# Attention over a cache with a gated unit: the split of the query rounds around the gate, and how four rows of w_o are shared among the DMA engines

## The chip, the cores and the metric

The kernel runs on one core of a Trainium2 chip. The core has five engines, each with its own queue of instructions: TensorE (PE in the profile, with weight loads as PEld), VectorE (DVE), ScalarE (ACT), GpSimd (POOL) and SyncE (SP). They work side by side and wait for each other through semaphores. Loads from device memory are issued by SP and ScalarE and carried out by 16 DMA engines. [...]

The metric is the device time of one execution in microseconds (us). The kernel before took 687.47 us, the median of three runs (687.0 to 690.81).

## What is computed

One token x of 512 values is normalized; xn then goes two ways. One is attention for 32 heads of 128 values over a cache of 8192 positions, the other a small gated unit whose result scales the attention's:

```python
def _A_ref(x, k_cache, v_cache, wq, wo):
    q = (x @ wq).reshape(B, Sq, H, Dh).transpose(0, 2, 1, 3)
    scores = jnp.einsum("bhqd,bhkd->bhqk", q, k_cache) * (Dh ** -0.5)
    p = _softmax(scores, axis=-1)
    o = jnp.einsum("bhqk,bhkd->bhqd", p, v_cache)
    return o.transpose(0, 2, 1, 3).reshape(B, Sq, H * Dh) @ wo
...
    xn = _layernorm(x, axis=-1)
    s = _A_ref(xn, A_k_cache, A_v_cache, A_wq, A_wo)
    g = _silu(_B_ref(xn, B_w_gate, B_w_up, B_w_down))   # (sigmoid(xn Wg) * (xn Wu)) Wd
    return x + s * g
```

All values are float32. The cache of keys and that of values are 128 MiB each; w_q and w_o are 8 MiB each. Every byte is used once, so the kernel is a stream of some 294 MB with little arithmetic on it.

## The kernel before

**Slots.** Three large slots of on-chip memory, A, B and C, hold what is loaded, one after another. C has w_q first, then the values of each pair of heads, and w_o at the end. A has the gated unit's weights first, then the keys of the odd pairs. B has the keys of the even pairs, and at the end the values of the last pair. A load into a slot can be issued only when the slot's last reader is done. Every load of the large slots is issued by SP, in program order, and its DMA queue works them off in that order.

**The beginning.** SP issues w_q (line 148), w_gate, w_up, w_down and the keys of pair 0 in two halves (152 to 156). ScalarE issues x twice and the last 96 rows of w_down (`wr`, 174). VectorE normalizes x. TensorE then computes all queries in eight rounds of 512 columns (`queries`, line 234): a round is four products with w_q that add up in one PSUM bank, and ScalarE copies it to `q_all` with two copies, one for each half of the partitions (245). A round yields the queries of two pairs of heads. Four rounds (banks 0 to 3) come ahead of the gated unit, four (banks 4 to 7) behind it.

Between them lies the gate. VectorE sums the weighted rows of w_gate and of w_up (`weighted`, 221); TensorE turns each of the two sums from a row over the partitions into a column (258, into the banks `turned`), ScalarE applies the sigmoid (263), VectorE multiplies (`hid`, 266) and sums the weighted rows of w_down (269 to 272). TensorE waits for ScalarE's last copy of the first rounds (276), adds up over the partitions into `g_ps` (bank 3, line 279), and ScalarE applies the sigmoid to `g_row` (283). The silu's other factor, `g_ps` itself, is multiplied in later by VectorE (367), behind the first pair's scores.

Two loads hang on this. The keys of pair 1 go into slot A and wait for the gate's last matmul (`sp.wait_ge(s_pe.sem, n_gate)`, 359). The values of pair 0 go into slot C and wait for the last round of queries (`sp.wait_ge(s_q, nq)`, 369).

**The pairs.** For each of the 16 pairs of heads VectorE computes the scores in two halves (`scores`, 295: a product with the query in place, 307, and a sum, 309), TensorE and VectorE find the maximum, ScalarE the exponentials (`softmax`, 317), and TensorE multiplies them with the values (`pair`, 336; line 350) into bank `po`, bank 0. SP issues the next keys when the scores have read the slot, the next values when `po` is done. `busy` (332) issues matmuls whose result nobody reads, into the gate's bank.

**The end.** When the values of pair 14 are used, SP issues w_o into slot C, in five transfers of all 128 partitions, each with its own semaphore (382):

```python
WO = ((0, 16), (16, 24), (24, 29), (29, 31), (31, 32))
...
for (r0, r1), c in zip(WO, d_wo):
    c.by(sp.dma_start(wo_t[:, r0:r1, :], wo.rearrange("(p r) e -> p r e", r=RW)[:, r0:r1, :]), 16)
```

Partition p holds 32 rows of w_o, each 2 KB; "rows 0 to 16" are the first 16 of each partition. TensorE waits for each transfer in turn (410) and multiplies its rows with the normalized attention `o_all`: rows 0 to 24 into one bank (414), which ScalarE copies (423) and TensorE folds in (427), and rows 24 to 32 into another (418). VectorE multiplies by `g_row` (431) and adds x (433), and SP sends the result out (435).

Of the kernel before, what the change touches and what calls it, by code (L numbers as in the profile page):

```python
# [9 lines left out]
P = 128  # L10
# [15 lines left out]
def kernel(  # L26
# [12 lines left out]
    pe, dve, act, pool, sp = nc.tensor, nc.vector, nc.scalar, nc.gpsimd, nc.sync  # L39
    _, H, S, Dh = k_cache.shape  # L40
# [5 lines left out]
    KT = D // P  # L46
    NG = 4
    GP = P // NG
    GC = D // NG
    SCALE = float(Dh) ** -0.5  # L50
    FP = F // P
    FL = F - FP * P
    QT = 512
    RW = H * Dh // P
# [17 lines left out]
    q_all = put("q_all", NP * Dh).rearrange("p (n d) -> p n d", d=Dh)  # L72
# [5 lines left out]
    ones = put("ones", P)  # L78
    x_row = put("x_row", GC)
    g_row = put("g_row", GC)  # L80
# [20 lines left out]
    xnb = o1.rearrange("p (k m) -> p k m", m=P)  # L101
# [4 lines left out]
    wq_t = C.rearrange("p (k c) -> p k c", k=KT)  # L106
    wo_t = C.rearrange("p (r e) -> p r e", e=D)

    psum = nc.alloc_psum_tensor("psum", [P, 8 * QT], F32).ap()
    bank = [psum[:, i * QT:(i + 1) * QT] for i in range(8)]  # L110
    po, pt, pm, g_ps, acc, fold_ps, o_ps, oTl = bank


    sems = []
# [1 line left out]
    def semaphore(name):  # L116
        sems.append(nc.alloc_semaphore(name))
        return sems[-1]

    names = "x xr wg wu wd wr wq ka k0 k1 kb va vb".split()  # L120
    d = {n: Count(semaphore(f"d_{n}")) for n in names}
    WO = ((0, 16), (16, 24), (24, 29), (29, 31), (31, 32))
    d_wo = [Count(semaphore(f"d_wo{i}")) for i in range(len(WO))]
    d_v = semaphore("d_v")
    s_dve, s_act, s_pe, s_pool = (Count(semaphore(n)) for n in ("s_dve", "s_act", "s_pe", "s_pool"))
# [48 lines left out]
    d["wr"].by(act.dma_start(wd_rest[:FL, :], w_down[FP * P:, :]), 16)  # L174
    dve.memset(st[:, 6:7], EPS)
    dve.memset(rs2, 0.0)
    for b in (4, 5):
        dve.memset(bank[b][:, :FP + 1], 0.0)
    dve.wait_ge(s_pool.sem, 2)
    for g in range(NG):  # L180
# [47 lines left out]
    n_xnb = s_dve.by(dve.tensor_copy(xnb, xn.rearrange("p (k o) -> p k o", o=1).to_broadcast([P, KT, P])))  # L228


    nq = H // NG
    n_qc = []

    def queries(lo, hi):
        with nc.Fori(lo, hi, engines=[pe.engine]) as t:
            for k in range(KT):
                m = pe.matmul(psum[:, bass.ds(t * QT, QT)], xnb[:, k, :], wq_t[:, k, bass.ds(t * QT, QT)],  # L237
                              start=(k == 0), stop=(k == KT - 1))
            m.then_inc(s_q, 1)
        for t in range(lo, hi):  # L240
            act.wait_ge(s_q, t + 1)
            pairs = slice(t * NG // 2, (t + 1) * NG // 2)
            for a in range(2):
                r = slice(a * HALF, (a + 1) * HALF)
                c = act.copy(q_all[r, pairs, :], bank[t][r, :].rearrange("p (n a d) -> p n a d", a=2, d=Dh)[:, :, a, :])
            n_qc.append(s_act.by(c))

    pe.wait_ge(d["wq"].sem, 16)
    pe.wait_ge(s_dve.sem, n_xnb)
    queries(0, nq // 2)  # L250

    turned = [bank[nq // 2 + a][:, :FP + 1] for a in range(2)]
    for a, (name, t) in enumerate((("wg", wg_t), ("wu", wu_t))):
        dve.wait_ge(d[name].sem, 16)
        weighted(t[:, 0, :], lambda k: t[:, k, :], lambda k: xn[:, k:k + 1], KT)
# [1 line left out]
        for i in range(FP):  # L257
            m = pe.matmul(turned[a][:, i:i + 1], t[:, 0, i:FP * P:FP], ones[:, 0:1], start=True, stop=True)
        m = pe.matmul(turned[a][:FL, FP:FP + 1], t[:, 0, FP * P:F], ones[:, 0:1], start=True, stop=True)
        n = s_pe.by(m)  # L260
# [12 lines left out]
                                             op0=ALU.mult, op1=ALU.add))  # L273
    pool.wait_ge(s_dve.sem, n_wr)
    n_prz = s_pool.by(pool.memset(prz.rearrange("p j a -> p (j a)"), 0.0))
    pe.wait_ge(s_act.sem, n_qc[-1])
    pe.wait_ge(s_dve.sem, n_wr)
    for g in range(NG):
        m = pe.matmul(g_ps[g * GP:g * GP + 1, :GC], ones[:, 0:1], wd_t[:, 0, g * GC:(g + 1) * GC],
                      start=True, stop=True)  # L280
    n_gate = s_pe.by(m)
    act.wait_ge(s_pe.sem, n_gate)
    n_gs = s_act.by(act.activation(g_row, g_ps[:, :GC], AF.Sigmoid))
    act.wait_ge(s_pool.sem, n_prz)
    queries(nq // 2, nq)


    def load_k(n, parts=1):
# [6 lines left out]
    def scores(n):  # L295
        kt = k_slot(n).rearrange("p (j d) -> p j d", d=Dh)
        s = sc[n % 2]
        h = NB // 2
        q = q_all[:, n:n + 1, :].to_broadcast([P, h, Dh])
        first = {0: d["ka"], NP - 1: d["kb"]}.get(n)  # L300
        if first:
            dve.wait_ge(first.sem, 16)
        for i in range(2):
            if i == bool(first):
                dve.wait_ge(k_sem(n).sem, 16 * (n // 2 + 1))
            part = kt[:, i * h:(i + 1) * h, :]
            s_dve.by(dve.tensor_mul(part, part, q))  # L307
            self_wait()
            s_dve.by(dve.reduce_sum(s[:, i * h:(i + 1) * h], part, axis=AX.X))  # L309
        k_free[n] = s_dve.n  # L310
        self_wait()
        dve.reduce_max(mx[:, 0:1], s, axis=AX.X).then_inc(s_rm, 1)
        dve.wait_ge(s_pt, n + 1)
        dve.reduce_max(mx[:1, 2:4], pt[:1, :P].rearrange("p (a m) -> p a m", a=2), axis=AX.X).then_inc(s_am, 1)  # L314
# [16 lines left out]

    def busy(count):
        for _ in range(count):
            pe.matmul(g_ps, ones, q_all[:, :QT // Dh, :], start=True, stop=True)

    def pair(v, waits, keep=(0, 0)):
        busy(keep[0])
# [23 lines left out]
    for n in range(NP):  # L361
        if n % (NG // 2) == 0:
            dve.wait_ge(s_act.sem, n_qc[n // (NG // 2)])
        scores(n)
        if n == 0:
            dve.wait_ge(s_act.sem, n_gs)
            s_dve.by(dve.tensor_mul(g_row, g_row, g_ps[:, :GC]))
        softmax(n)
    sp.wait_ge(s_q, nq)
    for n in range(NP - 1):  # L370
# [7 lines left out]
    for name, c in (("va", slice(0, SLOT // 2)), ("vb", slice(SLOT // 2, SLOT))):  # L378
        d[name].by(sp.dma_start(B[:, c], rows_of(v_src, NP - 1)[:, c]), 16)
    sp.wait_ge(s_po, NP - 1)  # L380
    for (r0, r1), c in zip(WO, d_wo):
        c.by(sp.dma_start(wo_t[:, r0:r1, :], wo.rearrange("(p r) e -> p r e", r=RW)[:, r0:r1, :]), 16)  # L382

    pe.wait_ge(s_act.sem, n_qc[-1])
    with nc.Fori(0, NP - 1, engines=[pe.engine], head_slot={pe.engine: 0}):
# [13 lines left out]
    n = s_dve.by(dve.transpose(o_turn, o_norm))  # L399
    pe.wait_ge(s_dve.sem, n)  # L400
    n = s_pe.by(pe.matmul(o_ps[:, :RW], turn, o_turn, start=True, stop=True))
    busy(1)
    dve.wait_ge(s_pe.sem, n)
    n = s_dve.by(dve.tensor_copy(o_all, o_ps[:, :RW]))
# [2 lines left out]
    pe.wait_ge(s_dve.sem, n)  # L407
    FOLD = WO[1][1]
    for (r0, r1), c in zip(WO, d_wo):
        pe.wait_ge(c.sem, 16)  # L410
        for r in range(r0, r1):
            if r < FOLD:
                g = r % NG
                m = pe.matmul(fold_ps[g * GP:g * GP + 1, :], o_all[:, r:r + 1], wo_t[:, r, :],
                              start=(r < NG), stop=(r >= FOLD - NG))
            else:
                for g in range(NG):
                    m = pe.matmul(acc[g * GP:g * GP + 1, :GC], o_all[:, r:r + 1],  # L418
                                  wo_t[:, r, g * GC:(g + 1) * GC], start=(r == FOLD), stop=(r == RW - 1))
        if r1 == FOLD:  # L420
            n = s_pe.by(m)
            act.wait_ge(s_pe.sem, n)
            n_f = s_act.by(act.copy(o1, fold_ps))
        if r1 == WO[2][1]:
            pe.wait_ge(s_act.sem, n_f)
            for g in range(NG):
                pe.matmul(acc[g * GP:g * GP + 1, :GC], sel, o1[:, g * GC:(g + 1) * GC], start=False, stop=False)  # L427
    n = s_pe.by(m)
# [4 lines left out]
    n = s_dve.by(dve.tensor_add(res, res, x_row))  # L433
# [35 lines left out]
```

## Time and profile before

| | |
|---|---|
| median of three runs | 687.47 us (687.0 to 690.81) |
| the profiled execution | 687.28 us |
| its span, first to last instruction | 685.4 us |
| moved by the DMA engines | 293.74 MB, mean 429 GB/s |
| TensorE, VectorE, ScalarE busy | 36%, 86%, 6% of the span |
| mean granted TensorE clock | 0.659 of full speed |

The profile comes from one execution. A row of its timeline has the start and length of a group of instructions in us, the engine (a "q" behind it means the engine's queue, where loads are issued), the line of the program, the operation, what it writes and reads, how many there are, and in brackets how long the engine sat idle before it and what ended that. A row of a table by stretches of time has the stretch and its length, the busy time of each engine with the number of its instructions, the granted clock of TensorE, the mean busy share of the 16 DMA engines and the rate at which they moved data. A packet counts in the stretch in which it starts, so shares over short stretches swing around their mean. A row on DMA issues has the size and the time from issue to landing.

### The profile page before, as it was taken

The page shows a single profiled execution, that of the slowest core. Times are in us where ns is not written, and L with a number is a line of the kernel's source. Part 1 is how long each engine was busy: PE and PEld are TensorE (multiplying, and loading weights), DVE is VectorE, ACT ScalarE, POOL GpSimd, SP SyncE. Part 2 cuts the span into 40 slices and gives each one's busy share as a digit, 9 for nine tenths or more (in the row PEclk, how much of TensorE's full clock was granted, in tenths as well). Part 3 has the DMA queues.
Part 4 walks back from the last instruction along what each step waited for, and adds up shares of the span by engine and source line. Part 5 has one row for each costly group of instructions (what it writes and reads, how often), then busy time and mean ns, then how long its engine had stood idle before and what let it go on. Part 6 is the DMA issues. An engine that isn't in the chain of part 4 may idle for free. (4 is left out here: it accounts for less than half of the span.)

```text
span 685.4 us, 3572 instructions
## 1 busy us (share of the span) xinstructions
PE 245.0 (36%) x1502; PEld 92.5 (14%) x1502; DVE 588.5 (86%) x145; ACT 41.5 (6%) x135; POOL 1.7 (0%) x10
## 2 busy tenths in 40 slices
PE   1595315050412405050422406060422406050486
PEld 0272101010110101010110101010110101010132
DVE  2259999999999999898989899898989899899930
ACT  0010110000000000000010100000010100000010
POOL 0000000000000000000000000000000000000000
PEclk9976856575665657575565757565665756565699
DMA  8999999999999999999999999999999999999996
GB/s 370 419 439 429 437 451 440 432 432 432 433 428 432 428 428 444 444 436 436 432 436 428 432 428 428 436 448 440 428 440 432 432 428 432 428 423 449 425 433 292
DMA packets 6501, 293.74 MB, mean 429 GB/s; under 512 B 760, under 2 KB 768, under 8 KB 1120
## 3 DMA queue, kind: packets, MB, share of 16 engines
q1 hardware_dynamic: 6344, 293.48, 99.1%
q10 hardware_dynamic: 152, 0.20, 0.1%
q8 instruction: 3, 0.05, 0.0%
q14 instruction: 2, 0.02, 0.0%
HBM read 293.67 MB, written 0.00 MB: 428 GB/s over the span
## 5 line engine op out<-in xcount | busy, mean ns | idle before, releaser
L307 DVE TENSOR_TENSOR slot<-slot,q_all 128x8192 f32<-128x8192 f32 x32 | 277.8, 8682 | 21.6 <-DMA slot<-in_A_k_cache_dram 21.6
L309 DVE TENSOR_REDUCE sc<-slot 128x64 f32<-128x8192 f32 x32 | 278.0, 8686 | 1.1
L350 PE MATMUL psum<-slot,prz 128*8 128x512 f32 x1024 | 143.9, 725 | 241.6 <-PEq L134 241.6
L350 PEld LDWEIGHTS psum<-slot,prz 128*8 128x8 f32 x1024 | 29.9, 102 | 342.0 <-issue 341.4
L339 PE MATMUL psum<-ident,mx 128*1 128x128 f32 x32 | 9.2, 387 | 119.4 <-PEq L134 119.4
L237 PE MATMUL psum<-slot,o 128*128 x64 | 32.1, 666 | 9.8 <-DMA slot<-in_A_wq_dram 9.8
L327 ACT COPY o<-psum 128x512 f32<-128x512 f32 x16 | 9.4, 586 | 397.6 <-PE psum L350 397.6
L355 PE MATMUL psum<-pick,o 128*128 128x2 f32 x128 | 16.4, 250 | 12.8 <-PEq L134 12.8
L355 PEld LDWEIGHTS psum<-pick,o 128*128 128x128 f32 x128 | 15.5, 191 | 27.2 <-issue 27.2
L339 PEld LDWEIGHTS psum<-ident,mx 128*1 128x1 f32 x32 | 1.8, 80 | 121.8 <-issue 121.8
L237 PEld LDWEIGHTS psum<-slot,o 128*128 128x128 f32 x64 | 13.6, 217 | 27.1 <-issue 27.1
L344 PE MATMUL psum<-rs,ones 128*128 128x2 f32 x32 | 8.7, 342 | 22.3 <-PEq L134 22.3
L222 DVE TENSOR_SCALAR slot<-slot,xn 128x1376 f32<-128x1376 f32 x2 | 1.9, 936 | 15.5 <-DMA slot<-in_B_w_gate_dram 15.0
L314 DVE TENSOR_REDUCE mx<-psum 1x2 f32<-1x128 f32 x16 | 4.4, 278 | 12.1 <-PE psum L339 12.1
L323 ACT ACTIVATE prz<-sc,mx 64x128 f32<-64x128 f32 x32 | 13.0, 406 | 0.7
L431 DVE TENSOR_TENSOR sc<-g_row,psum 128x128 f32<-128x128 f32 x1 | 0.3, 290 | 13.1 <-PE psum L418 13.1
L319 ACT ACTIVATE mx<-psum 128x2 f32<-128x2 f32 x16 | 2.8, 173 | 143.2 <-PE psum L341 143.2
L341 PE MATMUL psum<-mx,ones 1*128 1x2 f32 x32 | 8.6, 336 | 7.4 <-PEq L134 7.4
L344 PEld LDWEIGHTS psum<-rs,ones 128*128 128x128 f32 x32 | 7.8, 305 | 23.9 <-issue 23.9
L225 DVE SCALAR_TENSOR_TENSOR slot<-slot,xn 128x1376 f32<-128x1376 f32 x6 | 9.9, 1652 | 0.2
L395 DVE RECIPROCAL heads<-heads 128x32 f32<-128x32 f32 x1 | 0.4, 355 | 11.1 <-ACT heads L329 11.1
L341 PEld LDWEIGHTS psum<-mx,ones 1*128 1x128 f32 x32 | 7.7, 297 | 14.7 <-issue 14.7
(67 smaller groups left out, 84.0 us busy)
## 6 DMA issues: line engine op xcount, KB each, us to landing
slot<-in_A_k_cache_dram SPq DMA_DIRECT2D x4, 4096.0 KB, 45.5
slot<-in_A_v_cache_dram SPq DMA_DIRECT2D x2, 4096.0 KB, 37.5
slot<-in_A_wo_dram SPq DMA_DIRECT2D x1, 4096.0 KB, 20.7
slot<-in_B_w_gate_dram SPq DMA_DIRECT2D x1, 2752.0 KB, 28.2
slot<-in_B_w_up_dram SPq DMA_DIRECT2D x1, 2752.0 KB, 34.3
slot<-in_B_w_down_dram SPq DMA_DIRECT2D x1, 2560.0 KB, 39.8
slot<-in_A_wo_dram SPq DMA_DIRECT2D x1, 2048.0 KB, 25.2
slot<-in_A_wo_dram SPq DMA_DIRECT2D x1, 1280.0 KB, 27.7
```

The source lines that it names most:

```text
L225: s_dve.by(dve.scalar_tensor_tensor(acc, t(k), col(k), acc, op0=ALU.mult, op1=ALU.add))
L237: m = pe.matmul(psum[:, bass.ds(t * QT, QT)], xnb[:, k, :], wq_t[:, k, bass.ds(t * QT, QT)], start=(k == 0), stop=(k == KT - 1))
L307: s_dve.by(dve.tensor_mul(part, part, q))
L309: s_dve.by(dve.reduce_sum(s[:, i * h:(i + 1) * h], part, axis=AX.X))
L314: dve.reduce_max(mx[:1, 2:4], pt[:1, :P].rearrange("p (a m) -> p a m", a=2), axis=AX.X).then_inc(s_am, 1)
L323: e = act.activation(prz[r, :, a], sc[n % 2][r, :], AF.Exp, bias=mx[r, 4 + a:5 + a], scale=SCALE, accum_out=rs2[r, a:a + 1])
L327: act.copy(o1, po).then_inc(s_o1, 1)
L339: pe.matmul(pt[:1, :P], mx[:, 0:1], ident, start=True, stop=True).then_inc(s_pt, 1)
L341: pe.matmul(pm[:, 0:2], ones[:1, :], mx[:1, 2:4], start=True, stop=True).then_inc(s_pm, 1)
L344: pe.matmul(oTl[:, 2:4], ones, rs2, start=True, stop=True)
L350: m = pe.matmul(po[g * GP:g * GP + 2 * ROWS, :], prz[:, j * ROWS:(j + 1) * ROWS, :], v[:, j * QT:(j + 1) * QT], start=(j < NG), stop=(j >= ...
L355: m = pe.matmul(oTl[:, 0:2], o1[:, b * Dh:(b + 1) * Dh], pick[:, 2 * b:2 * b + 2], start=(b == 0), stop=(b == ROWS - 1))
```

## The change

Two things are changed.

The queries: three rounds come ahead of the gate (banks 0 to 2), five behind it (banks 1 to 5, through the new argument `first`). The gate's sums go to bank 0, `po`, instead of bank 3, the columns of the two turned sums to banks 6 and 7 instead of 4 and 5, and the matmuls of `busy` to bank 3, now called `idle`. TensorE's wait for the last copy ahead of the gate is removed. The product of `g_row` and `g_ps` moves from behind the first pair's scores to the middle of them, ahead of their second half.

w_o: the first transfer has rows 0 to 12 of all 128 partitions instead of rows 0 to 16. Rows 12 to 16 follow in five more transfers: one of partitions 0 to 80, then four of twelve partitions each (80 to 92, 92 to 104, 104 to 116, 116 to 128). With five partitions per engine in the first and one in each of the others, that is nine partitions on each of twelve DMA engines, and five on each of the other four. All six count on the first transfer's semaphore, and TensorE waits for the sum.

```diff
-    po, pt, pm, g_ps, acc, fold_ps, o_ps, oTl = bank
+    po, pt, pm, idle, acc, fold_ps, o_ps, oTl = bank
+    g_ps = po
...
+    FEW = 4
     WO = ((0, 16), (16, 24), (24, 29), (29, 31), (31, 32))
...
-    for b in (4, 5):
+    for b in (6, 7):
         dve.memset(bank[b][:, :FP + 1], 0.0)
...
-    nq = H // NG
+    nq, n0 = H // NG, 3
...
-    def queries(lo, hi):
+    def queries(lo, hi, first):
         with nc.Fori(lo, hi, engines=[pe.engine]) as t:
             for k in range(KT):
-                m = pe.matmul(psum[:, bass.ds(t * QT, QT)], xnb[:, k, :], wq_t[:, k, bass.ds(t * QT, QT)],
-                              start=(k == 0), stop=(k == KT - 1))
+                m = pe.matmul(psum[:, bass.ds(t * QT - (lo - first) * QT, QT)], xnb[:, k, :],
+                              wq_t[:, k, bass.ds(t * QT, QT)], start=(k == 0), stop=(k == KT - 1))
...
-    queries(0, nq // 2)
-
-    turned = [bank[nq // 2 + a][:, :FP + 1] for a in range(2)]
+    queries(0, n0, 0)
+
+    turned = [bank[6 + a][:, :FP + 1] for a in range(2)]
...
-    pe.wait_ge(s_act.sem, n_qc[-1])
     pe.wait_ge(s_dve.sem, n_wr)
...
-    queries(nq // 2, nq)
+    queries(n0, nq, 1)
...
             s_dve.by(dve.reduce_sum(s[:, i * h:(i + 1) * h], part, axis=AX.X))
+            if n == i == 0:
+                dve.wait_ge(s_act.sem, n_gs)
+                s_dve.by(dve.tensor_mul(g_row, g_row, g_ps[:, :GC]))
...
-            pe.matmul(g_ps, ones, q_all[:, :QT // Dh, :], start=True, stop=True)
+            pe.matmul(idle, ones, q_all[:, :QT // Dh, :], start=True, stop=True)
...
         scores(n)
-        if n == 0:
-            dve.wait_ge(s_act.sem, n_gs)
-            s_dve.by(dve.tensor_mul(g_row, g_row, g_ps[:, :GC]))
         softmax(n)
...
+    wo_src = wo.rearrange("(p r) e -> p r e", r=RW)
+
+    def load_wo(c, r0, r1, p0=0, p1=P):
+        c.by(sp.dma_start(wo_t[p0:p1, r0:r1, :], wo_src[p0:p1, r0:r1, :]), 16)
+
     for (r0, r1), c in zip(WO, d_wo):
-        c.by(sp.dma_start(wo_t[:, r0:r1, :], wo.rearrange("(p r) e -> p r e", r=RW)[:, r0:r1, :]), 16)
+        few = FEW if r0 == 0 else 0
+        load_wo(c, r0, r1 - few)
+        if few:
+            load_wo(c, r1 - few, r1, 0, P - 4 * 12)
+            for p in range(P - 4 * 12, P, 12):
+                load_wo(c, r1 - few, r1, p, p + 12)
...
     for (r0, r1), c in zip(WO, d_wo):
-        pe.wait_ge(c.sem, 16)
+        pe.wait_ge(c.sem, c.n)
```

More of the change, by code (lines that the diff above doesn't have):

```diff
@@ L244, in queries @@
                 r = slice(a * HALF, (a + 1) * HALF)
-                c = act.copy(q_all[r, pairs, :], bank[t][r, :].rearrange("p (n a d) -> p n a d", a=2, d=Dh)[:, :, a, :])
+                c = act.copy(q_all[r, pairs, :], bank[first + t - lo][r, :].rearrange("p (n a d) -> p n a d", a=2, d=Dh)[:, :, a, :])
             n_qc.append(s_act.by(c))
```

## The prediction

> **What bounds the kernel now.** I read the page's slices first, then the rate of the DMA engines in stretches (the windows view: length, busy time of each engine, granted TensorE clock, DMA share, GB/s), then the end in order of time.
>
> ```profile
> span 685.4 us, 3572 instructions
> DMA  8999999999999999999999999999999999999996
> GB/s 370 419 439 429 437 451 440 432 432 432 433 428 432 428 428 444 444 436 436 432 436 428 432 428 428 436 448 440 428 440 432 432 428 432 428 423 449 425 433 292
> ```
>
> The DMA engines are at 90% or more in 38 of 40 slices; only the first and the last are lower. The next rows say whether any stretch between has a hole.
>
> ```profile
> 9.89:12.31 2.42, 0.60 (x2) 0.50 (x2) 0.56 (x3) 0.00 (x0) 0.00 (x0) 1.00 1.00 433
> 43.10:61.40 18.30, 9.49 (x43) 7.97 (x44) 10.97 (x14) 0.46 (x2) 0.31 (x1) 0.50 0.99 430
> 61.40:80.80 19.40, 13.71 (x30) 5.63 (x29) 19.36 (x3) 2.94 (x8) 0.00 (x0) 0.94 1.01 436
> 100.10:640.00 539.90, 166.16 (x1092) 55.50 (x1092) 506.06 (x87) 26.64 (x98) 0.00 (x0) 0.61 1.00 435
> ```
>
> 430 to 436 GB/s everywhere: one stream of loads without a hole, and nothing but fewer bytes or a better ending can shorten it. The ending:
>
> ```profile
> 652.06 2.23 SPq L382 DMA_DIRECT2D slot<-in_A_wo_dram  x5
> 669.72 0.19 DVE L404 COPY o_all<-psum 128x32 f32<-128x32 f32 x1 [0.50 <-PE psum L401]
> 672.88 7.03 PE L414 MATMUL psum<-slot,o_all 128*1 128x512 f32 x48 [2.26 <-DMA slot<-in_A_wo_dram]
> 680.68 1.27 PE L418 MATMUL psum<-slot,o_all 128*1 128x128 f32 x40 [0.77 <-DMA slot<-in_A_wo_dram]
> 682.50 0.10 PEld L418 LDWEIGHTS psum<-slot,o_all 128*1 128x1 f32 x8 [0.18 <-DMA slot<-in_A_wo_dram]
> 683.03 0.29 DVE L431 TENSOR_TENSOR sc<-g_row,psum 128x128 f32<-128x128 f32 x1 [13.12 <-PE psum L418]
> ...
> 680.00:680.50 0.50, 0.00 (x0) 0.00 (x0) 0.00 (x0) 0.50 (x1) 0.00 (x0) 1.00 0.53 205
> 680.50:681.00 0.50, 0.32 (x12) 0.31 (x16) 0.00 (x0) 0.06 (x1) 0.00 (x0) 1.00 0.31 123
> 681.00:681.50 0.50, 0.50 (x28) 0.47 (x21) 0.00 (x0) 0.00 (x0) 0.00 (x0) 1.00 0.16 61
> 681.50:682.00 0.50, 0.50 (x29) 0.47 (x22) 0.00 (x0) 0.00 (x0) 0.00 (x0) 1.00 0.25 70
> 682.00:682.50 0.50, 0.50 (x25) 0.31 (x14) 0.00 (x0) 0.00 (x0) 0.00 (x0) 1.00 0.01 4
> ```
>
> TensorE waits for w_o before its first matmul (2.26 us), before row 24 (0.77) and before row 31 (0.18), so it follows the landings, and the end follows TensorE. The half-microseconds show what those landings wait for. 435 GB/s over 16 engines is 27.2 GB/s each; 205 GB/s after 680.0 are 7.5 engines still moving data, 123 are 4.5, then 61 and 70 are two or three. About ten engines have finished by 680.5, and the transfer counts as landed when the last one has, near 682.4. So the end waits some two microseconds for a handful of **late engines**.
>
> **Part one: three rounds of queries ahead of the gate.**
>
> ```profile
> 37.09 0.75 ACT L245 COPY q_all<-psum 64x256 f32<-64x256 f32 x2 [2.68 <-PE psum L237]
> 38.08 5.03 DVE L225 SCALAR_TENSOR_TENSOR slot<-slot,xn 128x1376 f32<-128x1376 f32 x3
> 40.52 0.75 ACT L245 COPY q_all<-psum 64x256 f32<-64x256 f32 x2 [2.68 <-PE psum L237]
> 44.97 4.65 PE L258 MATMUL psum<-ones,slot 128*128 128x1 f32 x20
> 50.05 0.17 DVE L266 TENSOR_TENSOR hid<-sg,psum 128x11 f32<-128x11 f32 x1 [6.94 <-PE psum L259]
> 58.75 0.61 PE L279 MATMUL psum<-slot,ones 128*1 128x128 f32 x8 [8.81 <-DVE slot L272]
> 59.29 15.82 PE L237 MATMUL psum<-slot,o 128*128 x32
> 59.42 0.33 SPq L292 DMA_DIRECT2D slot<-in_A_k_cache_dram  x1
> 59.42 0.28 ACT L283 ACTIVATE g_row<-psum 128x128 f32<-128x128 f32 x1 [14.10 <-PE psum L279]
> 67.24 8.69 DVE L309 TENSOR_REDUCE sc<-slot 128x64 f32<-128x8192 f32 x1
> 75.14 0.33 SPq L373 DMA_DIRECT2D slot<-in_A_v_cache_dram  x1
> 94.54 0.26 DVE L367 TENSOR_TENSOR g_row<-g_row,psum 128x128 f32<-128x128 f32 x1
> ```
>
> A round costs 40.52 - 37.09 = 3.43 us of TensorE. Without the fourth one the turning of the gate's sums starts 3.43 us sooner, and the second turning (44.97 now) is then bound by VectorE, whose w_up sum ends at 38.08 + 5.03 = 43.11. So hid, the gate and the load of the second pair's keys (59.42), which stands behind the gate on SP's queue, all come 44.97 - 43.15 = 1.8 us sooner: keys issued at 57.6. The wait of TensorE for the last query copy goes too; those copies are done by 41.3 (40.52 + 0.75), long before the gate, so it costs nothing today.
>
> What is that worth? The keys' data follow the first pair's without a hole: 430 GB/s up to 61.40, 436 after. An issue 1.98 us ahead of its turn was already early enough. I take **0 us**. It would gain if that lead were sometimes too short; the bound is the 1.8 us.
>
> The price is behind the gate. Five rounds instead of four end 3.43 us later after a start 1.8 us sooner, so the first values are issued at 75.14 + 1.6 = 76.8. Their turn comes at 80.80, 4.0 us later, and the keys needed no more than 1.98: it is covered, with 2.0 us to spare. On ScalarE one round's copies (0.75 us) move behind the gate; their first user is the scores of pair 6, many loads later. The product of g_row (0.26 us, at 94.54 now) moves in between the two halves of the first scores on VectorE, where the first sum ends at 67.24 + 8.69 = 75.9; queued behind it is the second half, which gains 1.8 and loses 0.26, and the wait it brings, on ScalarE's sigmoid, has been over for 16 us by then (59.42 + 0.28). The new banks and the idle matmuls in another bank cost nothing: same shapes, same count. Sum of part one: 0.
>
> **Part two: the dealt rows.** w_o's first transfer is 4096 KB for 16 rows, 2 KB per row and partition, so four rows are 8 KB of each partition, 0.30 us of one engine (8.2 KB at 27.2 GB/s).
>
> ```profile
> slot<-in_A_wo_dram SPq DMA_DIRECT2D x1, 4096.0 KB, 20.7
> slot<-in_A_wo_dram SPq DMA_DIRECT2D x1, 256.0 KB, 28.6
> ```
>
> Today each engine has 8 of 128 partitions. Twelve get a ninth: +0.30 us. Four fall to five: -0.90 us. The last transfer is issued at 653.9 (652.06 + 2.23 less its own 0.43) and lands 28.6 us on, at 682.4. If the four are the latest, they end at 681.5. The others then decide: with 4.5 engines at work in 680.5 to 681.0 and two or three in the next half, a fifth may run to about 681.4, and +0.30 makes 681.7. The gain is 0.7 us, less some 0.1 for ten more small packets and five more completions on each engine: **-0.6 us**. TensorE can use it, since its three waits all end with a landing and o_all is ready at 669.91, 2.9 us before the first use. Five more issues on SP, at 0.45 us each (2.23 / 5), run to 656.5 and nothing stands behind them but the output. w_o's 32 rows of 256 KB need 19.3 us at 435 GB/s, so until about 661 the engines still move the last values, and the issues are hidden.
>
> The unknown is whether transfers of 80 and 12 partitions move at the rate of 128. Only one load in the trace has another count: 96 partitions of w_down, beside w_q.
>
> ```profile
> wd_rest<-in_B_w_down_dram ACTq DMA_DIRECT2D x1, 192.0 KB, 22.3
> ...
> 12.31:14.80 2.49, 1.18 (x4) 1.00 (x4) 0.76 (x5) 0.26 (x1) 0.00 (x0) 1.00 1.00 432
> 14.80:17.34 2.54, 0.00 (x0) 0.00 (x0) 0.78 (x3) 0.00 (x0) 0.00 (x0) 1.00 0.99 423
> 17.34:19.94 2.60, 0.00 (x0) 0.00 (x0) 0.00 (x0) 0.00 (x0) 0.00 (x0) 1.00 1.00 416
> 19.94:22.53 2.59, 0.00 (x0) 0.00 (x0) 0.00 (x0) 0.00 (x0) 0.00 (x0) 1.00 1.00 418
> 22.53:27.00 4.47, 2.82 (x4) 1.27 (x5) 0.00 (x0) 0.00 (x0) 0.00 (x0) 1.00 1.03 412
> ```
>
> Against 433 GB/s the five stretches lose 0.01 + 0.06 + 0.10 + 0.09 + 0.22 = 0.47 us for 192 KB. If all of it comes of the odd partition count, the dealt 1024 KB cost 5.3 times as much, 2.5 us. If it comes of two queues alternating on each engine (this load is ScalarE's queue, the rest SP's; the dealt rows are all SP's), they cost nothing; the first stretch, where the load is already under way, loses next to nothing. The bounds are 0 and 2.5. I take 0, the nearer to every row of SP's queue alone, and keep 2.5 as a rival.
>
> [...]
>
> **The sum.** The profiled execution took 687.28 us, 1.9 more than its span, and stands 0.2 under the median of the runs (687.47). 687.28 + 0 - 0.6 = **686.7 us**.
>
> **The rivals.**
>
> Crowding (chance 0.28). Twelve engines writing twelve neighbouring partitions get in each other's way, and an engine that must do its descriptors in order can't use the time. The loss of rate beside the 96-partition load speaks for it; the first of those stretches speaks against. Its price is 2.5 us on the twelve, which have no slack, on top of their +0.30: 687.28 + 2.8 = 690.1, slower than before. It decides as soon as it costs more than the 0.9 us that the four engines are relieved by. [...]
>
> The four engines aren't the late ones (0.10). The windows count engines, they don't name them. Then a late one gets a ninth partition: 687.28 + 0.3 + 0.1 = 687.7.
>
> The keys' lead is too short outside the profiled execution (0.07). A stream with a hole at 61.4 would gain up to 1.8 us from part one: 687.28 - 0.6 - 1.8 = 684.9. Against it: 436 GB/s with no dip.
>
> **How the numbers follow.** The forecast has 0.55. A difference of 0.5%, 3.4 us, is about what a measurement of this kernel can tell from no change; from 687.47 that is under 684.0 or over 690.9. Only the last rival at its full price comes near the first: faster 0.02. Of crowding's 0.28 about 0.10 lies over 690.9: slower 0.11 with a stray hundredth. The rest, 0.87, is the same. The range runs from 685.7, which cuts off most of the last rival, to 690.8, which leaves out crowding's upper third.
>
> **What would show it.** Right: the rate stays at 430 to 436 GB/s across 61.4; the keys are issued near 57.6 and the first values near 76.8; the half-microseconds at the end fall off together instead of trailing at two or three engines; the last w_o row lands near 681.8. Wrong: a stretch well under 420 GB/s at 665 to 675, where the dealt rows flow, with the first w_o wait of TensorE longer than 2.26 us (crowding); a tail as long as now (other engines late); a dip at 80.8, because the five rounds ran over 2.0 us longer than worked out, as they would on a clock that stays at the 0.50 of the stretch before 61.40.

## The result and the profile after

| | before | after |
|---|---|---|
| median of 7 runs, us | 687.14 | 692.0 |
| lowest to highest, us | 686.91 to 690.81 | 691.28 to 693.35 |
| profiled execution, us | 687.28 | 691.28 |
| its span, us | 685.4 | 689.4 |

The changed kernel takes 1.007 of the time before, 95% interval 1.0052 to 1.0087: 4.9 us more, where 0.6 us less were forecast. In the profiled executions the difference is 4.00 us. Here and below, executions over 1.5% above the fastest of their kernel (701 to 807 us) are left out of medians, ranges and ratios, and the ratios with their intervals are worked out from all the executions that remain, not from the two medians.

The page of the changed kernel, its span and two of its slice rows:

```profile
span 689.4 us, 3581 instructions
...
DMA  8999999999999999999999999999999999999997
GB/s 368 416 436 461 446 426 426 430 426 430 445 453 434 426 430 426 430 426 464 437 430 430 426 430 426 456 445 430 426 430 430 426 445 453 407 426 456 420 366 254
```

The DMA engines are as busy as before in every slice, up to the last. Only the bytes moved differ, and only at the end: 366 and 254 GB/s where there were 433 and 292. A share of busy time can't show this loss; the rate does. The windows view of the same kernel (length, busy time of each engine, granted TensorE clock, DMA share, GB/s) cuts it out:

```profile
61.40:80.80 19.40, 14.74 (x35) 6.25 (x33) 19.36 (x4) 3.67 (x10) 0.00 (x0) 0.99 1.00 432
100.10:640.00 539.90, 167.54 (x1092) 55.86 (x1092) 504.18 (x87) 26.61 (x98) 0.00 (x0) 0.61 1.00 435
...
666.00:668.00 2.00, 1.20 (x14) 0.79 (x8) 0.00 (x0) 0.58 (x1) 0.00 (x0) 1.00 0.92 389
668.00:670.00 2.00, 1.85 (x8) 0.92 (x8) 0.93 (x4) 0.16 (x1) 0.00 (x0) 1.00 1.03 254
670.00:672.00 2.00, 0.73 (x2) 0.00 (x0) 0.01 (x1) 0.00 (x0) 0.00 (x0) 1.00 1.14 180
672.00:674.00 2.00, 0.00 (x0) 0.00 (x0) 0.00 (x0) 0.00 (x0) 0.00 (x0) 1.00 1.22 172
674.00:676.00 2.00, 0.00 (x0) 0.00 (x0) 0.00 (x0) 0.00 (x0) 0.00 (x0) 0.63 0.71 193
676.00:678.00 2.00, 0.86 (x8) 0.18 (x12) 0.00 (x0) 0.00 (x0) 0.00 (x0) 0.50 1.05 434
...
668.00:676.00 8.00, 2.58 (x9) 0.92 (x8) 0.95 (x4) 0.16 (x1) 0.00 (x0) 0.91 1.03 200
```

The same stretch of the kernel before:

```profile
668.00:676.00 8.00, 5.59 (x28) 1.50 (x31) 0.95 (x4) 0.16 (x1) 0.00 (x0) 0.87 0.94 404
```

For eight microseconds, in which the dealt rows flow, the stream runs at 200 GB/s, and then it is back at 434. The missing (404 - 200) x 8.00 us = 1.63 MB take 3.75 us at 435 GB/s, of the 4.00 that the execution is longer. The trace shows a full DMA share (1.03) all the while: the packets take longer, the engines don't wait between them.

The end of the changed kernel, in the timeline and then in half-microseconds:

```profile
652.38 4.27 SPq L385 DMA_DIRECT2D slot<-in_A_wo_dram  x10
...
677.14 7.40 PE L426 MATMUL psum<-slot,o_all 128*1 128x512 f32 x48 [6.41 <-DMA slot<-in_A_wo_dram]
684.66 1.27 PE L430 MATMUL psum<-slot,o_all 128*1 128x128 f32 x40
...
687.03 0.29 DVE L443 TENSOR_TENSOR sc<-g_row,psum 128x128 f32<-128x128 f32 x1 [17.01 <-PE psum L430]
```

```profile
684.50:685.00 0.50, 0.38 (x19) 0.33 (x18) 0.00 (x0) 0.38 (x1) 0.00 (x0) 1.00 0.70 270
685.00:685.50 0.50, 0.50 (x28) 0.48 (x20) 0.00 (x0) 0.20 (x1) 0.00 (x0) 1.00 0.16 61
685.50:686.00 0.50, 0.50 (x28) 0.46 (x24) 0.00 (x0) 0.00 (x0) 0.00 (x0) 1.00 0.25 61
686.00:686.50 0.50, 0.50 (x26) 0.29 (x16) 0.00 (x0) 0.00 (x0) 0.00 (x0) 1.00 0.00 0
```

TensorE's first wait for w_o grew from 2.26 to 6.41 us, and its first matmul on w_o starts at 677.14 instead of 672.88, 4.26 us later. What stands behind follows at about that distance: the product with `g_row`, near the end, starts 4.00 us later (687.03 for 683.03). The last two or three engines (61 GB/s) still trail for a microsecond.

### The profile page after: what moved, and what is told of

Read it like the earlier page. It is cut to its first block, busy times and chain, and to the rows that moved or that the text cites. A ratio compares the mean times of both kernels' runs of the same rounds, so it can differ in the third digit from the quotient of the medians.

```text
span 689.4 us, 3581 instructions
## 1 busy us (share of the span) xinstructions
PE 247.1 (36%) x1502; PEld 92.8 (13%) x1502; DVE 588.6 (85%) x145; ACT 41.4 (6%) x135; POOL 1.7 (0%) x10
## 2 busy tenths in 40 slices
DMA packets 6693, 293.74 MB, mean 426 GB/s; under 512 B 824, under 2 KB 832, under 8 KB 1184
## 5 line engine op out<-in xcount | busy, mean ns | idle before, releaser
L354 PE MATMUL psum<-slot,prz 128*8 128x512 f32 x1024 | 145.4, 732 | 252.6 <-PEq L136 252.6
L359 PEld LDWEIGHTS psum<-pick,o 128*128 128x128 f32 x128 | 15.5, 191 | 27.2 <-issue 27.2
```

The lines of the kernel that those rows point to most:

```text
L354: m = pe.matmul(po[g * GP:g * GP + 2 * ROWS, :], prz[:, j * ROWS:(j + 1) * ROWS, :], v[:, j * QT:(j + 1) * QT], start=(j < NG), stop=(j >= ...
L359: m = pe.matmul(oTl[:, 0:2], o1[:, b * Dh:(b + 1) * Dh], pick[:, 2 * b:2 * b + 2], start=(b == 0), stop=(b == ROWS - 1))
```

## The experiments

The first theory was the rival of the prediction, crowding: the engines of a small transfer write few neighbouring partitions and get in each other's way. Against it stood the unequal shares (nine partitions and five), the number of transfers, the reading side and, later, the place: that an engine is fast only on the partitions that it also has in a transfer of 128. Variants that ran together on one chip are compared with the same executions of the kernel before, so its median differs a little from group to group. The variants of w_o's load all keep the four and four rounds of queries of the kernel before, and have `load_wo` and the wait on `c.n` as the change has them; the diffs show only what stands under `if few:` (rows 12 to 15, 1024 KB).

### One part at a time

The queries alone, which is the changed kernel with no dealt rows:

```diff
-    FEW = 4
+    FEW = 0
```

> The changed kernel with the query rounds three and five, but w_o in its five ordinary transfers. Theory crowding (the dealt transfers cost the time, because neighbouring partitions are written by many engines at once): 687.1, no change against the kernel before, keys issued near 57.5, first values near 76.2, rate 435 GB/s in 100 to 640 us. Rival queries (the five rounds behind the gate cost something, by the later values or the moved product): 690 to 692 here. If the keys' lead was sometimes too short, up to 1.8 us faster than before, 685.3.

Measured: 686.84 us against 687.04, ratio 0.9997 (0.9988 to 1.0006). The windows of this kernel:

```profile
61.40:80.80 19.40, 15.67 (x36) 6.47 (x35) 19.36 (x4) 3.67 (x10) 0.00 (x0) 0.99 1.00 432
...
668.00:676.00 8.00, 6.01 (x27) 1.75 (x30) 0.95 (x4) 0.16 (x1) 0.00 (x0) 0.80 0.97 416
```

The order of the queries is worth nothing, and no hole comes or goes at 61.4 or 80.8.

The deal alone, with the loop of the change:

```diff
+        if few:
+            load_wo(c, r1 - few, r1, 0, P - 4 * 12)
+            for p in range(P - 4 * 12, P, 12):
+                load_wo(c, r1 - few, r1, p, p + 12)
```

> The kernel before with its four and four query rounds, and only the dealt rows of w_o. Theory crowding: the whole loss is here, 691 to 692 (4.0 to 4.9 us over before), with the rate near 150 GB/s while the four transfers of twelve partitions flow and the first w_o wait of TensorE ending near 677. Rival queries: 687 to 688.

Measured: 691.4 against 687.04, 1.0066 (1.005 to 1.0081). This kernel's window:

```profile
668.00:676.00 8.00, 2.45 (x8) 0.79 (x7) 0.95 (x4) 0.16 (x1) 0.00 (x0) 0.92 1.04 223
```

The deal alone loses 4.4 us, and as far as the intervals tell that is the whole loss.

### Equal shares, next to each other and apart

```diff
+        if few:
+            for p in range(0, P, 16):
+                load_wo(c, r1 - few, r1, p, p + 16)
```

> The kernel before, rows 12 to 16 of w_o in eight transfers of sixteen neighbouring partitions each (0 to 16, 16 to 32 and so on): every engine keeps 8 partitions. [...] Theory count (each additional small transfer costs a fixed time, 4.0 us for five more = 0.8 us each): seven more transfers, 692.5. Theory share (the twelve engines with nine partitions are the cost): every engine has eight, so 687.1.

```diff
+        if few:
+            for p in (0, 1, 2, 3, 64, 65, 66, 67):
+                c.by(sp.dma_start(wo_t[p:p + 61:4, r1 - few:r1, :], wo_src[p:p + 61:4, r1 - few:r1, :]), 16)
```

> The kernel before, rows 12 to 16 in eight transfers of sixteen partitions each, but taken at a step of four (0, 4, 8 to 60; 1, 5 to 61; and so on, then the same from 64): the same number of transfers, bytes and engines as with sixteen neighbours. [...] Theory count: the same as the neighbours, 692.5. Theory share: 687.1.

Measured: 692.11 (1.0076, 1.006 to 1.0091) and 690.93 (1.0054, 1.0039 to 1.007), against 687.04. The window of the first, then that of the second:

```profile
668.00:676.00 8.00, 2.48 (x8) 0.82 (x7) 0.95 (x4) 0.16 (x1) 0.00 (x0) 0.77 1.06 211
```

```profile
668.00:676.00 8.00, 3.11 (x8) 0.82 (x7) 0.95 (x4) 0.16 (x1) 0.00 (x0) 0.62 1.01 280
```

Each of these transfers has sixteen more packets under 512 B (888 for 760 in both traces), which fits sixteen engines with one partition each. With eight partitions to every engine nothing is won back, so unequal shares aren't the cause. Spreading the partitions helps, 280 for 211 GB/s, but 3.9 of the 5.1 us stay where no two neighbours are in one transfer: crowding alone doesn't account for them.

### Count, bytes and size of the transfers

Four more transfers, of all 128 partitions and one row each:

```diff
+        if few:
+            for r in range(r1 - few, r1):
+                load_wo(c, r, r + 1)
```

> The kernel before, rows 12 to 16 of w_o in four transfers, one for each row, all of 128 partitions. Theory crowding: no change, 687.1 to 687.4, since every transfer is spread as the ordinary ones are. Theory count (a fixed 0.8 us for each additional transfer): four more, 690.3. Theory share: 687.1.

The deal of the change for two rows instead of four:

```diff
-    FEW = 4
+    FEW = 2
```

> The kernel before with rows 14 to 16 dealt (two rows instead of four, the same six transfers, half the bytes). Theory crowding: the loss goes with the bytes, half of that with four rows, 689 to 689.6. Theory count: the loss goes with the number of transfers and stays whole, 691 to 692. If relieving four engines gains something beside the crowding, a little less than half.

Two transfers, of 80 and 48 partitions, none of twelve:

```diff
+        if few:
+            load_wo(c, r1 - few, r1, 0, 80)
+            load_wo(c, r1 - few, r1, 80, P)
```

> The kernel before, rows 12 to 16 in two transfers, of partitions 0 to 80 and 80 to 128: five and three partitions on every engine, eight in all. [...] Theory count: one more transfer, 687.9. Theory share: every engine has eight partitions, 687.1. A loss well under that with four transfers of twelve says that most of it comes from those.

The 80 kept, the twelves four partitions apart:

```diff
+        if few:
+            load_wo(c, r1 - few, r1, 0, 80)
+            for p in range(80, 84):
+                c.by(sp.dma_start(wo_t[p:p + 45:4, r1 - few:r1, :], wo_src[p:p + 45:4, r1 - few:r1, :]), 16)
```

> The kernel before with the dealt rows, where each of the four transfers takes twelve partitions at a step of four (80, 84 to 124; 81 to 125; and so on) instead of twelve neighbours: the same engines, bytes and number of transfers. [...] Theory count and theory share: as with the neighbours, 691 to 692.

Measured, against 687.07, with the GB/s of 668 to 676 from the rows below:

| | us | ratio (95%) | GB/s |
|---|---|---|---|
| four single rows | 687.23 | 1.0004 (0.9994 to 1.0014) | 425 |
| two rows dealt | 689.5 (688.04 to 690.78) | 1.0037 (1.0026 to 1.0048) | 320 |
| 80 and 48 | 691.18 | 1.006 (1.0044 to 1.0077) | 265 |
| 80 and twelves apart | 692.97 (690.09 to 698.33) | 1.0114 (1.0072 to 1.0155) | 240 |

The windows of the four kernels, one fence each, in the order of the table:

```profile
668.00:676.00 8.00, 6.00 (x28) 1.83 (x31) 0.95 (x4) 0.16 (x1) 0.00 (x0) 0.79 1.03 425
```

```profile
668.00:676.00 8.00, 4.31 (x18) 0.95 (x20) 0.95 (x4) 0.05 (x1) 0.00 (x0) 0.84 0.99 320
```

```profile
668.00:676.00 8.00, 2.62 (x9) 0.96 (x8) 0.95 (x4) 0.16 (x1) 0.00 (x0) 0.80 1.04 265
```

```profile
668.00:676.00 8.00, 2.67 (x13) 1.05 (x16) 0.95 (x4) 0.16 (x1) 0.00 (x0) 0.95 1.01 240
```

Four more transfers of all 128 partitions cost nothing that shows, so the count alone isn't the cause. Half the bytes cost 0.37% for 0.66, about half, so the loss goes with the bytes. The third run was the surprise: two large transfers lose nearly as much as the change, though 48 partitions for sixteen engines are far less crowded than twelve for twelve. By crowding it should lose much less. The fourth is inconclusive: its four runs spread over 8 us, and its trace is of the fastest of them (690.09).

### The reading side, and a step that reaches almost everywhere

Sixteen neighbours again, read from one contiguous piece of w_o:

```diff
+        if few:
+            flat = wo.rearrange("(p r) e -> p r e", r=few)
+            for p in range(0, P, 16):
+                c.by(sp.dma_start(wo_t[p:p + 16, r1 - few:r1, :], flat[p:p + 16, :, :]), 16)
```

> As with sixteen neighbours, the same eight transfers to the same partitions, but read from one contiguous megabyte of w_o (8 KB from partition to partition instead of 64 KB), so that rows 12 to 16 hold other rows of w_o. Theory crowding (the writing side): the loss stays, 691.5 to 692.5. Rival reading (sixteen engines that read at a pitch of 64 KB get in each other's way at the source): the loss goes, 687 to 688.

Seven transfers of sixteen partitions, seven apart, and the last sixteen:

```diff
+        if few:
+            for p in range(7):
+                c.by(sp.dma_start(wo_t[p:p + 106:7, r1 - few:r1, :], wo_src[p:p + 106:7, r1 - few:r1, :]), 16)
+            load_wo(c, r1 - few, r1, 112, P)
```

> The kernel before, rows 12 to 16 in seven transfers of sixteen partitions at a step of seven (0, 7 to 105; 1 to 106; to 6 to 111) and one of the sixteen neighbours 112 to 128: again eight transfers, eight partitions on every engine. [...] Rival place (any engine that writes partitions other than those that it has in a transfer of 128 is slow, however they are spread): as with the step of four, 3 us later, 690 to 691. Rival count: 692.

Measured, against 686.95: 692.03 (1.0063, 1.0044 to 1.0082) and 691.16 (1.0056, 1.004 to 1.0072). The windows of the one and of the other:

```profile
668.00:676.00 8.00, 4.00 (x11) 1.60 (x11) 0.95 (x4) 0.16 (x1) 0.00 (x0) 0.60 1.03 211
```

```profile
668.00:676.00 8.00, 3.25 (x14) 1.59 (x14) 0.95 (x4) 0.16 (x1) 0.00 (x0) 0.96 0.99 253
```

211 GB/s with the other source, as without it: the loss isn't on the reading side. And the step of seven lost 4.2 us, though seven of its eight transfers have no neighbours; the place had 690 to 691, and 691.16 lies just above it. Spread thin is not enough.

### The 96 partitions of w_down

The row that the prediction had to read, w_down's rest: the same bytes on 128 partitions.

```diff
-    d["wr"].by(act.dma_start(wd_rest[:FL, :], w_down[FP * P:, :]), 16)
+    w_rest = w_down[FP * P:, :].rearrange("r e -> (r e)").rearrange("(p c) -> p c", p=P)
+    d["wr"].by(act.dma_start(wd_rest[:, :FL * D // P], w_rest), 16)
...
-    n_wr = s_dve.by(dve.scalar_tensor_tensor(wd_t[:FL, 0, :], wd_rest[:FL, :], hid[:FL, FP:FP + 1], wd_t[:FL, 0, :],
+    n_wr = s_dve.by(dve.scalar_tensor_tensor(wd_t[:FL, 0, :FL * D // P], wd_rest[:FL, :FL * D // P], hid[:FL, FP:FP + 1], wd_t[:FL, 0, :FL * D // P],
```

> The kernel before with w_o untouched; the 192 KB of w_down that ScalarE loads beside w_q go to 128 partitions of 384 values each instead of 96 of 512, so the last 96 rows of w_down are summed up from other values, over 384 columns. Theory crowding: the dip of the rate at 12 to 27 us (433 down to 412 to 418 GB/s) is gone or under a third, and the stream, with everything behind it, is some 0.3 to 0.45 us sooner: 686.7 against 687.1. Rival queues (two queues that alternate on each engine make the dip): the dip stays and the time too.

Measured: 686.61 against 686.95, 0.9994 (0.9985 to 1.0003). The stretch beside this load, in the kernel before and then with 128 partitions:

```profile
12.31:27.00 14.69, 4.00 (x8) 2.28 (x9) 1.53 (x7) 0.26 (x1) 0.00 (x0) 1.00 1.01 419
```

```profile
12.31:27.00 14.69, 4.62 (x8) 2.52 (x9) 1.56 (x8) 0.26 (x1) 0.00 (x0) 1.00 1.01 435
```

It is still ScalarE's queue beside SP's, and the dip is gone: (435 - 419) x 14.69 us = 235 KB, 0.54 us. So it came of the form with 96 partitions, not of the two queues. (Each partition's piece shrinks with it from 2 KB to 1.5 KB; that was not tried apart.) The time itself, 0.3 us less, is within the interval; the reading rests on the rate, which is 419 GB/s in the trace of the changed kernel as well.

### In place and out of place

Two kernels that differ in nothing but the partitions that are written: eight transfers of eight partitions, four apart, 512 KB in all, on partitions 0 to 63 in the first and 64 to 127 in the second. They are called in place and out of place after an assumption of the author's about which engine writes which partition; the profile doesn't name the engine of a packet, so no run shows it.

```diff
+        if few:
+            for p in (0, 1, 2, 3, 32, 33, 34, 35):
+                c.by(sp.dma_start(wo_t[p:p + 29:4, r1 - few:r1, :], wo_src[p:p + 29:4, r1 - few:r1, :]), 16)
```

> The kernel before, rows 12 to 16 in eight transfers of eight partitions at a step of four (0, 4 to 28; 1, 5 to 29; and so on to 35, 39 to 63); the rows 12 to 16 of partitions 64 to 128 are left out. [...] Theory place (an engine is fast on its own partitions and slow on others): no loss, eight engines do what they did before and eight have less to do, 685.5 to 687.2, packets of 8 KB at 0.31 us each. Rival shape (whatever isn't 128 partitions is slow): half of the bytes of the sixteen-partition runs, 1.5 to 2.5 us more, 688.5 to 689.5.

```diff
-            for p in (0, 1, 2, 3, 32, 33, 34, 35):
+            for p in (64, 65, 66, 67, 96, 97, 98, 99):
```

> The same eight transfers of eight partitions at a step of four, but of partitions 64 to 128 (64, 68 to 92, and so on to 99, 103 to 127); those of partitions 0 to 64 are left out. [...] Theory place: slow, 1.5 to 2.5 us more than in place, 687.5 to 689.5, with the rate well under 400 GB/s from 668 to 673. Rival shape: the same time as in place.

The run in place has 825 packets under 512 B and the run out of place 824, for 760 of the kernel before: eight more for each of the eight transfers (and one in the run in place), which fits eight engines. Which eight they are isn't shown.

Measured, against 687.05: in place 686.33 (0.9992, 0.9982 to 1.0002), out of place 689.78 (1.005, 1.0033 to 1.0067). The windows of the run in place, and below them its timeline at TensorE's first matmul on w_o:

```profile
668.00:673.00 5.00, 3.75 (x21) 1.24 (x24) 0.95 (x4) 0.16 (x1) 0.00 (x0) 1.00 1.02 431
```

```profile
671.81 3.61 PE L425 MATMUL psum<-slot,o_all 128*1 128x512 f32 x32 [1.10 <-DMA slot<-in_A_wo_dram]
```

And the same two views of the run out of place:

```profile
668.00:673.00 5.00, 2.35 (x7) 0.69 (x6) 0.95 (x4) 0.16 (x1) 0.00 (x0) 1.00 1.00 220
```

```profile
675.25 8.26 PE L425 MATMUL psum<-slot,o_all 128*1 128x512 f32 x48 [4.75 <-DMA slot<-in_A_wo_dram]
```

Same bytes, same shape, same step, same number of transfers; 431 GB/s in one and 220 in the other, and 3.45 us between them. If only the packets of a small transfer hindered each other, the two would be alike. What decides is **the place**: with these transfers on partitions 0 to 63 the stream keeps its rate, with the same transfers on 64 to 127 it goes at half.

### Why the place matters: what the other engines do

Two theories were left. Either a transfer out of place is slow by itself (one), or it is slow because other engines write at the same time (two), as if a way into the memory were taken twice. An estimate speaks for the second: 220 is half of 435, as if sixteen engines had the ways of eight. Three kernels load rows 8 to 15 on 32 partitions alone, in eight transfers of eight, and leave them out on the other 96: on partitions 0 to 31, 4 to 35, and 64 to 95. The names of the runs follow the same assumption as before, and "engines 0 to 7" in the expectations are the eight that do these transfers; the numbers are the author's.

```diff
-    FEW = 4
+    FEW = 8
...
+            for r in (r1 - few, r1 - few // 2):
+                for p in (0, 1, 2, 3):
+                    c.by(sp.dma_start(wo_t[p:p + 29:4, r:r + few // 2, :], wo_src[p:p + 29:4, r:r + few // 2, :]), 16)
```

> [...] Engines 0 to 7 have 64 KB less each, 2.4 us at 27.2 GB/s. Both theories: no loss from the small transfers, 684.3 to 685.0 us (687.1 - 2.4), and the rate stays over 400 GB/s while they flow.

```diff
-                for p in (0, 1, 2, 3):
+                for p in (4, 5, 6, 7):
```

> [...] Theory one, an engine is slow wherever it is out of place: as the run of eight out of place, 2.4 to 3.5 us over the run in place, 687 to 688.5, and a rate of 200 to 280 GB/s while the transfers flow. [...]

```diff
-                for p in (0, 1, 2, 3):
+                for p in (64, 65, 66, 67):
```

> [...] Both theories: 2.4 to 3.5 us over the run in place, 687 to 688.5. [...]

Measured, against 686.95: 684.41 in place (0.9975, 0.9955 to 0.9995), 686.7 rotated (0.9986, 0.9962 to 1.001), 687.44 on the other half (1.0019, 0.9996 to 1.0042). The rotated runs scatter, from 685.3 to 689.38, where those in place lie between 683.73 and 687.67. The windows of the three, in this order:

```profile
667.00:672.00 5.00, 4.47 (x26) 2.02 (x30) 0.95 (x4) 0.40 (x2) 0.00 (x0) 1.00 1.00 428
```

```profile
667.00:672.00 5.00, 3.34 (x14) 1.71 (x14) 0.95 (x4) 0.26 (x2) 0.00 (x0) 1.00 1.03 360
```

```profile
667.00:672.00 5.00, 3.34 (x14) 1.71 (x14) 0.95 (x4) 0.26 (x2) 0.00 (x0) 1.00 0.95 218
```

The other half gives 218 GB/s, half of 435. The rotated run gives 360, more than theory one's 200 to 280, and its median is 2.3 us over the run in place, near theory one's 2.4. Yet the rotated run and the other half differ in nothing but the partitions, 4 to 35 and 64 to 95, and they move 360 and 218, so one price for being out of place doesn't give both. Why the rotated run loses at all these runs don't show. Hence the same pair with all sixteen rows, 128 KB for each of the eight engines (an estimate: 4.8 us at 27.2 GB/s, and as much less than before):

```diff
-    FEW = 8
+    FEW = 16
...
+        if not few:
+            load_wo(c, r0, r1)
         if few:
+            for r in range(r0, r1, 4):
+                for p in (0, 1, 2, 3):
+                    c.by(sp.dma_start(wo_t[p:p + 29:4, r:r + 4, :], wo_src[p:p + 29:4, r:r + 4, :]), 16)
```

> [...] Engines 0 to 7 have 4.8 us less to do, and then TensorE's own nine microseconds after o_all bind: 683 to 684.5 us. The rate is over 410 GB/s from 664 to 670.

The rotated kernel has (4, 5, 6, 7) in place of (0, 1, 2, 3):

> As the long run in place, but rotated by one (partitions 4 to 35); rows 0 to 15 of the other 96 partitions are left out. Theory one, an engine out of place is slow by itself, at about half: engines 0 to 7 then give 109 GB/s for 218, so 300 to 360 GB/s all through 664 to 670, and an end about 4.8 us over the run in place, 686 to 689. [...]

Measured, against 687.1: 682.62 in place (0.9943, 0.9927 to 0.996) and 683.29 rotated (0.9945, 0.9927 to 0.9962). The timeline of SP's queue in the long run in place, and below it this run's windows:

```profile
653.16 10.79 SPq L395 DMA_DIRECT2D slot<-in_A_wo_dram  x16
664.00 1.98 SPq L385 DMA_DIRECT2D slot<-in_A_wo_dram  x4
```

```profile
660.00:662.00 2.00, 2.00 (x24) 0.51 (x20) 0.00 (x0) 0.00 (x0) 0.00 (x0) 1.00 0.57 229
662.00:664.00 2.00, 2.00 (x24) 0.55 (x20) 0.00 (x0) 0.00 (x0) 0.00 (x0) 1.00 0.52 213
...
658.00:664.00 6.00, 5.68 (x48) 1.61 (x51) 0.00 (x0) 1.05 (x5) 0.00 (x0) 1.00 0.71 300
```

And windows of the long rotated run:

```profile
660.00:662.00 2.00, 2.00 (x24) 0.53 (x20) 0.00 (x0) 0.00 (x0) 0.00 (x0) 1.00 0.48 184
662.00:664.00 2.00, 2.00 (x24) 0.39 (x19) 0.00 (x0) 0.00 (x0) 0.00 (x0) 1.00 0.50 205
...
658.00:664.00 6.00, 5.68 (x48) 1.44 (x50) 0.00 (x0) 0.89 (x4) 0.00 (x0) 1.00 0.72 299
```

Neither run went as laid out: sixteen small transfers take SP 10.79 us to issue, so from 660 to 664 the other eight engines have nothing to do and about half the engines work (share 0.52 and 0.50 from 662 to 664). That makes the plainest comparison of all. From 662 to 664 eight engines move 213 GB/s on partitions 0 to 31, and 205 on partitions 4 to 35. From 660 to 662 the rotated run is further below, 184 for 229, but a packet counts where it starts: over 658 to 664 the two are alike, 299 for 300. Theory one has 109 in the four microseconds behind 660, an estimate of some 230 over these six. And the rotated run ends 0.67 us later by the medians, where theory one had 4.8. So partitions 4 to 35 aren't slow by themselves.

What these runs didn't try is the long rotated run beside eight engines at work: when those start, the dealt rows are nearly through (1 MB takes 4.9 us at 213 GB/s). Nor did any transfer to partitions 64 to 127 run alone. What is shown is this: with partitions 4 to 35 the stream goes at 360 GB/s for 428 while all the engines are at work (share 1.03), and at 205 for 213 while about half of them are (0.50 and 0.52); with partitions 64 to 95, beside all the engines, it goes at 218. That transfers are slow out of place **because others write at the same time** is the reading that fits these rates; what they share, and a further cost of the place itself, the runs don't show.

The other runs aren't worked out from it. Why sixteen neighbours (211 GB/s), and four and seven partitions apart (280 and 253), lose 5.1, 3.9 and 4.2 us isn't derived from any run: that the cause is the same is argued. That 96 partitions cost a little (419 GB/s) may be of the same kind; that too is argued.

Whether relieving the late engines is worth anything by itself wasn't measured: every deal run here slowed the stream, to 200 to 320 GB/s from 668 to 676. Nearest to it comes the run of eight in place, in which eight engines have 64 KB less each and none has more. Its end, in half-microseconds:

```profile
681.00:681.50 0.50, 0.50 (x24) 0.28 (x12) 0.00 (x0) 0.00 (x0) 0.00 (x0) 1.00 0.14 41
681.50:682.00 0.50, 0.42 (x12) 0.10 (x8) 0.00 (x0) 0.00 (x0) 0.00 (x0) 1.00 0.00 0
```

The last data come about half a microsecond sooner than before (70 GB/s there from 681.5 to 682.0), and one or two engines still trail; the time, 0.7 us less, is within its interval, and 512 KB less were loaded.

## Why the prediction was wrong, point by point

**What bounds the kernel** held. The end followed the landings of w_o: +4.26 us at TensorE's first matmul on it, +4.00 in the execution's time. That the rate is 430 to 436 GB/s "everywhere" is contradicted by the prediction's own later rows, 412 to 423 between 14.80 and 27.00, and the price of the 96 partitions lay in them.

**Part one at 0** was right, and so were its steps, to within 0.6 us. The timeline of the changed kernel:

```profile
43.06 4.69 PE L260 MATMUL psum<-ones,slot 128*128 128x1 f32 x20 [1.21 <-DVE slot L227]
...
48.18 0.17 DVE L268 TENSOR_TENSOR hid<-sg,psum 128x11 f32<-128x11 f32 x1 [5.17 <-PE psum L261]
...
57.46 0.33 SPq L293 DMA_DIRECT2D slot<-in_A_k_cache_dram  x1
...
76.17 0.33 SPq L374 DMA_DIRECT2D slot<-in_A_v_cache_dram  x1
```

The second turning is bound by VectorE, as worked out (43.06 for 43.15); hid comes 1.87 us sooner for 1.8; the keys are issued at 57.46 for 57.6 and the first values at 76.17 for 76.8, since the five rounds took 18.81 us and not 15.82 + 3.43. The rate across 61.4 and 80.8 is 432 GB/s. Work was moved by almost two microseconds, and nothing waited for it.

**SP's five further issues** were hidden, as said: 652.38 + 4.27 = 656.65, and the dealt rows don't flow before about 667. The four single rows confirm it at no cost.

**The relief of the late engines, -0.6 us,** was never seen. After the change the rate still falls to 61 GB/s for the last microsecond, as it did before, where it should have fallen off at once. But while the dealt rows flowed the stream went at half its rate, so the runs can't tell what the relief alone would be worth; it stays open. The 0.1 us in this term, for more packets and completions, is shown by no run. What the trace shows is 192 packets more in all (6693 for 6501), 64 of them under 512 B, as the sixteen engines of one transfer and the twelve of four would give; that these are the same twelve each time isn't shown. The four single rows, four more transfers for every engine, changed the time by 0.2 us (687.23 for 687.07), which is within their interval.

**The step that failed** is this one: "The bounds are 0 and 2.5. I take 0, the nearer to every row of SP's queue alone, and keep 2.5 as a rival." Its reason was a reading of the rows beside the 96-partition load: "If it comes of two queues alternating on each engine [...] they cost nothing". The run with w_down's rest on 128 partitions shows the other reading, the partitions: still two queues, and no dip. The term put at 0 measured 4.4 us, by the deal alone. "SP's queue alone" was also no resemblance that counted: every load on SP has 128 partitions, and in this the 96 were the nearest row. The upper bound was too small as well: 2.5 us carried 0.47 us for 192 KB over to 1024 KB, and the change lost 4.9. Nor does a price per KB carry over: for the same 1024 KB the runs have from 0.2 us (four single rows) to 5.1 (sixteen neighbours).

**The rival crowding** had the sign, the window and the signs to look for: a stretch under 420 GB/s at 665 to 675, with a wait over 2.26 us. Its size was too small, +2.8 us for 4.9, and its chance of 0.28 followed from the reading that failed. As a mechanism it counted the twelve engines of one transfer against each other; the same form of transfer moving 431 or 220 GB/s by its partitions alone isn't in it. That an engine which is held up must keep its order is shown by no run.

**The other rivals.** Whether the four are the late ones can't be seen behind the loss. That the keys' lead is too short fell with the queries alone: 686.84 against 687.04.

No kernel run here that does the whole work beats the one before by more than its interval; the three that do (684.41, 682.62 and 683.29 us) leave out rows of w_o.

## What to carry to other kernels

Where one stream of loads bounds a kernel, look at the rate and not at the share of busy DMA engines, which stood at 1.03 while half the bandwidth was gone. Split such loads by rows, with all 128 partitions in each transfer, which cost nothing that shows here (687.23 us for 687.07); the load dealt by hand cost 4.4 us. And where a cost has two bounds, and one row has the same odd feature, start from that row, not from the many that lack it.

## What was not expected of the hardware

Transfers of eight partitions slow the whole stream or don't, by the partitions that they write: 218 GB/s on 64 to 95, 428 on 0 to 31. A load of 96 partitions on ScalarE's queue took the stream from 435 to 419 GB/s. And SP's time for an issue differs with the form of the transfers, from 0.43 us each in the change (4.27 / 10) to 0.67 in the long run in place (10.79 / 16), where the five of the kernel before took 2.23 / 5 = 0.45. What makes the difference stays open.
